# Early half expert with one PSUM bank and one product per attention iteration, four score banks throughout, and two loads moved ahead of the weights

## Chip, core and metric

The kernel runs on one core of a Trainium2 chip. The metric is the device time of one execution in microseconds (us); lower is better. TensorE is called PE here (PEld is its weight load), VectorE DVE, ScalarE ACT, GpSimd POOL; SP is the engine that issues most DMAs.

## What is computed

A causal attention with a decay bias, a mixture of eight experts that every token visits with its own weight, and a feed-forward block, one after the other, in float32.

```python
scores = scale * np.matmul(q, k.transpose(0, 1, 3, 2))        # 2 batches, 8 heads, 576 x 576, head_dim 64
scores = np.where(causal, -1000000000.0, scores + np.minimum(bias, 0.0))
attn = softmax(scores)
x = (attn @ v) as [1152, 512]
P = exp(x @ w_gate), then 8 rounds of row and column normalisation
for e in range(8):
    out += P[:, e:e + 1] * (np.maximum(x @ w1[e], 0.0) @ w2[e])     # 512 -> 1024 -> 512
h = out @ w_in                                                  # 512 -> 2048
y = (np.maximum(h, 0.0) + np.log1p(np.exp(-np.abs(h)))) @ w_out
```

## The kernel before

Every matrix is split into a high and a low part (`hi` rounded by ACT, `lo` the remainder on DVE or POOL) and every product is three matmuls on these parts. An expert's 1024 hidden units are handled as two half experts of 512, so the loop `for x in range(NH)` runs over 16 half experts and then 4 pieces of the feed-forward block. The tokens are two groups `g` of 576 (the two batches). For an expert, the first matrix product of a group is made by seven block products (Strassen's scheme, `Unit.product`, line 313, six matmuls of 288 columns each, into a PSUM tile `ph`); sums of them, relu and split give `hh` and `hl`. The second product, `downs` (line 449), takes tiles of 128 tokens: four steps of three 512-column matmuls into a PSUM tile `py`, which is then added to `acc`.

The attention comes first. Its unit is a pair of heads `p` (0 to 7, the first `NP` = 4 are batch 0) and a block `i` of 128 queries (0 to 3, and 4 for the last 64 rows of both heads). There are 40 units, and the loop over `n` is a software pipeline: iteration `n` issues the scores of unit n+1 (`do_S`), the transposes of unit n-3 (`do_T`), their copies to SBUF of unit n-4 (`do_V`), the product with v of unit n-5 (`do_A`), the softmax of unit n with the norm of unit n-2 (`do_B`, DVE), and the exponentials of unit n (`do_E`, ACT). The string `"YSKAXVWBMTED"` is the order in which these are written, so it sets the order on every engine's queue. Three more entries fill the pipeline: `W` prepares expert weights (`early_w`), `Y` builds the split x of group 0 from the finished attention of batch 0 (`build`), and `M` steps `early`, the generator of the first half expert's group 0 (`lone_half`, `Unit.lone`), from iteration 29 on.

PSUM has eight banks. Two (`tr`) hold transposes. `ring_bank` hands out the score banks: `s0`, `s1`, `s2`, `y0` in turn for pairs 0 to 3, but only the first three for pairs 4 to 7, two per unit; `y0` then holds `pv` (attention times v). `y1` and `y2` go to the early half expert: `lone` accumulates one chain of products in `y1` and puts the others in `y2`, copying partial sums from `y1` to the SBUF tile `xt`.

The loads of q and k for a pair (`load_qk`) go through SP's DMA queue, in the tiles `qk`, of which there are four. Pair 2's are issued when pair 0's last scores have been written, behind the four weight loads of 512 KB (`load`, line 158) and pair 1's v. `split_qk` makes the parts `kh`, `kl`, `qh`, `ql`; `split_ends` copies the last 64 columns of `qh` and `ql` to `end0h`... by DMA.

After the loop, `build` runs for group 1 while the rest of `early` is stepped, and the remaining steps go through `step()`. `step()` is called after each piece of the expert loop, and for x < 2 it advances `gates` (`gate_steps`) once in three calls and, from the seventh time on, once in seven. `gates` is the normalisation of P: a small matmul `pcs` (line 938) and some twelve DVE instructions on `gate`, `gs` and `csr` a round. What is left of it when x = 1 ends is run at once there (`for _ in gates: pass`).

Of the kernel before, what the change touches and what calls it, by code (L numbers as in the profile page):

```python
# [20 lines left out]
def attention_moe_ffn(ctx, tc, q, k, v, s, w_gate, w1, w2, w_in, w_out, out):  # L21
    nc = tc.nc
# [40 lines left out]
    def f(ap):  # L63
        return ap.bitcast(F32)
# [232 lines left out]
    class Unit:  # L297
# [23 lines left out]
        def lone(self):  # L321

            relu, sub = AF.Relu, ALU.subtract
            p = self.p

            def copy(n):
                nc.vector.tensor_copy(xt[:, n, :], a)

            def total_(n, z, m):
                nc.vector.tensor_tensor(out=xt[:, n, :], in0=z, in1=xt[:, m, :], op=ALU.add)  # L330

            def high(z, q, cols):
                nc.scalar.activation(out=hb[0][:, q, cols], in_=z, func=relu)

            def low(z, q, cols):
                nc.vector.scalar_tensor_tensor(out=hb[1][:, q, cols], in0=z, scalar=0.0, in1=f(hb[0][:, q, cols]),
                                               op0=ALU.max, op1=sub)

            a = bank("y1", "ph")[:, :HB]
            self.product(a, A11, B11, True)  # L340
            yield
            copy(0)
            b = bank("y2", "ph")[:, :HB]
            self.product(b, A12, B21, True)
            yield
            self.product(a, S2, T2, False)
            total_(2, b, 0)
            yield
            copy(1)
            high(xt[:, 2, :], p, self.h0)  # L350
            c = bank("y2", "ph")[:, :HB]
            self.product(c, S3, T3, True)
            yield
            self.product(a, S1, T1, False)
            low(xt[:, 2, :], p, self.h0)
            yield
            copy(0)
            total_(3, c, 0)
            self.product(a, S4, B22, False)
            yield  # L360
            high(xt[:, 3, :], p + 2, self.h1)
            self.product(c, A22, T4, False)
            high(a, p, self.h1)
            low(xt[:, 3, :], p + 2, self.h1)
            yield
            low(a, p, self.h1)
            total_(2, c, 1)
            high(xt[:, 2, :], p + 2, self.h0)
            low(xt[:, 2, :], p + 2, self.h0)

# [60 lines left out]

    def downs(x, groups):

        for tiles in groups:
            py = {}
            for t in tiles:
                nd[0] += 1
                py[t] = ps.tile([P, DM], F32, tag=f"y{1 + nd[0] % 2}", name="py", bufs=1)
            if x == XE:
# [34 lines left out]

    def lone_half():
        for p in range(2):
            yield from Unit(0, p, 0).lone()
            yield
        yield from downs(0, A_GROUPS)

    with tc.manual_schedule():
# [13 lines left out]
        with ExitStack() as att:  # L495
# [12 lines left out]
            def load_qk(n):  # L508

                p, r = divmod(n, 2)  # L510
                if p >= B * NP:
                    return
                b, hp = divmod(p, NP)
                x = ap2.tile([P, S], F32, tag="qk", name="qk", bufs=4)
                nc.sync.dma_start(out=x, in_=(q if r else k)[b, hp])
                qk_t.append(x)
# [108 lines left out]
            def scores(u):  # L625
                p, i = u
                t = pair.get(p)
                sc = [ring_bank("sc", 4 if p < NP else 3) for _ in range(2)]
                live[u] = dict(sc=sc)
# [24 lines left out]
            load_bias(1)  # L654
            nc.sync.dma_start(out=c8d, in_=f(cs))
            for which in (1, 2):
                for i in range(2):
                    load(0, which, i)
# [90 lines left out]
            def attend(u):  # L749
# [4 lines left out]
                if i == 0:  # L754
                    t["pv"] = bank("y1" if p < NP else "y0", "pv")
                if i < NB:
# [38 lines left out]
            def do_S(n):  # L795
                if unit(n + 1):
                    p, i = unit(n + 1)
                    scores((p, i))
                    if i == (0 if p else NB):
                        load_qk(2 * p + 4)  # L800
                        load_qk(2 * p + 5)
# [21 lines left out]
            def do_Y(n):  # L823
                for _ in range(3):
                    while building and next(building[0], 1):
                        building.pop(0)
# [19 lines left out]
            def do_D(n):  # L846
                if unit(n):
                    p, i = unit(n)
                    if i == NB - 1:
                        split_ends(p + 1)  # L850

            def do_W(n):
                for _ in range(0 if n < 9 else 1 if n < EARLY - 4 else 2):
                    next(prework, None)

            EARLY = NP * (NB + 1) + 9

            def do_M(n):
                for _ in range(0 if n < EARLY else 1 if n < nu + 3 else 2):
                    next(early, None)  # L860

            do = dict(S=do_S, T=do_T, V=do_V, A=do_A, X=do_X, Y=do_Y, B=do_B, E=do_E, K=do_K, D=do_D, W=do_W, M=do_M)
            for n in range(nu + LA + LX + 1):
                now[0] = n
                for x in "YSKAXVWBMTED":
                    do[x](n)
# [167 lines left out]
        def step(z=""):  # L1034
# [4 lines left out]
            if x < XE:  # L1039
                if tick[1] >= (3 if tick[3] < 6 else 7) and tick[2] > 2 and not dense[0]:  # L1040
                    next(gates, None)
                    tick[1] = 0
                    tick[3] += 1
# [146 lines left out]
```

## Time and profile before

| | us |
|---|---|
| three runs | 1117.37, 1120.87, 1120.93 |
| median | 1120.87 |
| profiled execution, device time | 1117.36 |
| its span (first to last instruction) | 1115.6 |
| busy in the span: PE, PEld, DVE, ACT, POOL | 1078.1, 953.1, 777.3, 517.5, 360.7 |

The span is cut into stages below by the start of a pair's first scores on PE: pair 1 at 16.40 us, pair 2 at 34.76, then 46.16, 57.56, 74.76, 91.50 and 110.09 for pair 7. The attention's last PE work ends near 141 us, and the experts and the feed-forward block fill the rest.

### The profile page before, as it was taken

The numbers are of one execution on the slowest core, as the hardware profiler recorded it, in microseconds if no ns is written. First come the engines' busy times: TensorE is split into PE (matmuls) and PEld (weight loads), VectorE is DVE, ScalarE is ACT, GpSimd is POOL, SyncE is SP. The second block draws the span as 40 slices with busy tenths as digits, with TensorE's granted clock in tenths as the row PEclk, the third lists the DMA queues.
The fourth block names the chain that finished last, engine by engine and source line by source line (L and its number), as shares of the span: only waits on it lengthen the run. The fifth ranks groups of instructions, "written<-read, shape, count | busy, mean of one in ns | idle before, by whom it ended". The sixth has DMA issues, their size and how long they took to land.

```text
span 1115.6 us, 18099 instructions
## 1 busy us (share of the span) xinstructions
PE 1078.1 (97%) x6692; PEld 953.1 (85%) x6692; DVE 777.3 (70%) x1727; ACT 517.5 (46%) x1227; POOL 360.7 (32%) x426
## 2 busy tenths in 40 slices
PE   5988999989999999999999999999999999999998
PEld 3766788878989899899989989889898889989997
DVE  5555464676877787887878888885545559687874
ACT  4887534332443343443433434434333357565662
POOL 5775321203424142342424324142130023233231
PEclk9999999999999999999999999999999999999999
DMA  5220201111323213232122312222011210121002
GB/s 191 72 73 31 71 2 38 38 49 65 130 79 114 96 67 111 79 133 95 67 95 95 132 66 97 95 76 85 20 57 38 76 39 1 41 74 38 1 1 85
DMA packets 30425, 78.50 MB, mean 70 GB/s; under 512 B 6048, under 2 KB 10656, under 8 KB 30336
## 3 DMA queue, kind: packets, MB, share of 16 engines
q1 hardware_dynamic: 27768, 68.93, 18.3%
q0 software_dynamic: 2560, 8.39, 1.9%
q8 instruction: 53, 0.87, 0.3%
q14 instruction: 36, 0.29, 0.1%
q10 hardware_dynamic: 8, 0.01, 0.0%
HBM read 66.00 MB, written 10.82 MB: 69 GB/s over the span
## 4 chain that ended last, share of the span: by engine, by line
PE 92%; DVE 4%; ACT 2%; DMA 1%; issue 1%; POOL 1%; ACTq 0%; POOLq 0%
PE py L449 43%; PE ph L313 32%; PE ph L424 9%; PE sc L647 2%; PE pv L759 2%; PE tr L733 1%; PE sc L651 1%; PE pv L769 1%; PE tr L727 1%; DVE xl L104 1%; DMA qk<-in_k 1%; ACT pt L747 1%; PE pg L915 0%; ACT eb L702 0%; ACT xh L101 0%
## 5 line engine op out<-in xcount | busy, mean ns | idle before, releaser
L449 PE MATMUL py<-w2h,hh 128*128 128x512 f32 x720 | 284.4, 395 | 1.9 <-DVE acc L464 1.6
L449 PE MATMUL py<-w2h,hl 128*128 128x512 f32 x720 | 282.6, 392 | 1.3 <-DVE hl L261 1.3
L449 PE MATMUL py<-w2l,hh 128*128 128x512 f32 x720 | 283.8, 394 | 0.0
L313 PE MATMUL ph<-xh,w1h 128*128 128x288 f32 x896 | 265.9, 297 | 0.0
L313 PE MATMUL ph<-xl,w1h 128*128 128x288 f32 x896 | 264.9, 296 | 0.0
L313 PE MATMUL ph<-xh,w1l 128*128 128x288 f32 x896 | 264.9, 296 | 0.0
L313 PEld LDWEIGHTS ph<-xh,w1h 128*128 128x128 f32 x896 | 168.8, 188 | 18.4 <-issue 1.7
L313 PEld LDWEIGHTS ph<-xl,w1h 128*128 128x128 f32 x896 | 169.0, 189 | 15.6
L318 ACT ACTIVATE xt<-ph 128x288 f32<-128x288 f32 x186 | 74.8, 410 | 206.0 <-PE ph L313 199.4
L313 PEld LDWEIGHTS ph<-xh,w1l 128*128 128x128 f32 x896 | 169.1, 189 | 0.0
L449 PEld LDWEIGHTS py<-w2h,hl 128*128 128x128 f32 x720 | 135.1, 188 | 33.5 <-DVE hl L261 2.4
L258 ACT ACTIVATE hh<-ph 128x288 fp32r<-128x288 f32 x186 | 76.0, 410 | 161.0 <-DVE ph L410 81.5
L449 PEld LDWEIGHTS py<-w2h,hh 128*128 128x128 f32 x720 | 135.1, 188 | 15.4 <-DVE acc L464 2.0
L449 PEld LDWEIGHTS py<-w2l,hh 128*128 128x128 f32 x720 | 135.1, 188 | 10.5
L224 POOL TENSOR_TENSOR w2l<-raw,w2h 128x512 fp32r<-128x512 f32 x40 | 56.2, 1405 | 269.7 <-ACT w2h L222 269.7
L467 DVE SCALAR_TENSOR_TENSOR acc<-py,gate,acc 128x512 f32<-128x512 f32 x126 | 93.9, 746 | 52.8 <-PE py L449 52.8
L998 POOL TENSOR_TENSOR cm<-cm,ct 128x512 f32<-128x512 f32 x32 | 44.9, 1402 | 209.3 <-DVE ct L996 209.3
L172 DVE TENSOR_TENSOR w1l<-raw,w1h 128x512 fp32r<-128x512 f32 (+1 forms) x144 | 98.5, 684 | 13.5 <-ACT w1h L169 13.3
L261 DVE SCALAR_TENSOR_TENSOR hl<-ph,hh 128x288 fp32r<-128x288 f32 x186 | 83.9, 453 | 29.7 <-ACT hh L258 28.1
L281 POOL TENSOR_TENSOR a<-a,a 128x288 f32<-128x288 f32 x64 | 51.7, 808 | 124.0 <-DVE a L279 121.8
L169 ACT ACTIVATE w1h<-raw 128x512 fp32r<-128x512 f32 (+1 forms) x144 | 82.9, 576 | 1.6 <-PE ph L313 1.6
L424 PE MATMUL ph<-xh,w1h 128*128 128x288 f32 x256 | 75.8, 296 | 0.0
(185 smaller groups left out, 1695.4 us busy)
## 6 DMA issues: line engine op xcount, KB each, us to landing
raw<-in_w SPq DMA_DIRECT2D x64, 512.0 KB
f<-in_w_in SPq DMA_DIRECT2D x16, 512.0 KB
f<-in_w_out SPq DMA_DIRECT2D x16, 512.0 KB
wd<-cm POOLq DMA_DIRECT2D x32, 256.0 KB, 2.9
raw<-wd SPq DMA_DIRECT2D x16, 512.0 KB
qk<-in_k SPq DMA_DIRECT2D x8, 288.0 KB
qk<-in_q SPq DMA_DIRECT2D x8, 288.0 KB
out<-acc SPq DMA_DIRECT2D x9, 256.0 KB
```

Source lines behind the costliest of these rows:

```text
L169: nc.scalar.activation(out=hi[:, o], in_=t[:, src], func=AF.Copy)
L172: nc.vector.tensor_tensor(out=lo[:, o], in0=t[:, src], in1=f(hi[:, o]), op=ALU.subtract)
L224: (nc.gpsimd if i else nc.vector).tensor_tensor(out=lo, in0=t[:, r], in1=f(hi), op=ALU.subtract)
L258: nc.scalar.activation(out=hh, in_=z, func=AF.Relu)
L261: nc.vector.scalar_tensor_tensor(out=hl, in0=z, scalar=0.0, in1=f(hh), op0=ALU.max, op1=ALU.subtract)
L281: nc.gpsimd.tensor_tensor(out=a2, in0=a1, in1=a2, op=ALU.subtract)
L313: nc.tensor.matmul(o, u, v, start=(start and c == 0 and n == 0), stop=(c == 1 and n == 2), skip_group_check=True)
L318: nc.scalar.activation(out=t, in_=self.a, func=AF.Copy)
L424: nc.tensor.matmul(o, u, v, start=(n == 0), stop=(n == 11))
L449: nc.tensor.matmul(py[t], u, v, start=(k == 0 and n == 0), stop=(k == NF - 1 and n == 2))
L467: nc.vector.scalar_tensor_tensor(out=a, in0=py, scalar=gate_t[0][:, t, e:e + 1], in1=a, op0=ALU.mult, op1=ALU.add)
L998: nc.gpsimd.tensor_tensor(out=m, in0=m, in1=f(t), op=ALU.add)
```

## The change

`lone` no longer accumulates in PSUM over several products: each of the seven products goes to bank `y2`, and its result is copied or added into one of four SBUF tiles `xt` by DVE. A `yield` now stands between the product and its eviction, and `M` stands twice in the string, ahead of `T` and behind it. So an iteration evicts the previous product in its first `M` and issues the next one in its second, behind the transposes; it starts at iteration 30. The scores use all four ring banks for every pair, and `pv` is always in `y1`. The down products of the early half take one tile at a time, with the banks `y2`, `y2`, `y1`, `y2`. Pair 2's q and k are loaded before the weights; for this pair 0's q and k lie in the buffers of `kh` and `qh`. `Y` takes two steps an iteration in place of three, `W` goes to two steps from iteration 28 in place of 25, and `step()` advances `gates` once in six calls in place of seven.

```diff
         def lone(self):
-            a = bank("y1", "ph")[:, :HB]
-            self.product(a, A11, B11, True)
-            yield
-            copy(0)
-            b = bank("y2", "ph")[:, :HB]
-            self.product(b, A12, B21, True)
-            yield
-            self.product(a, S2, T2, False)
-            total_(2, b, 0)
...
+            p, h0, h1 = self.p, self.h0, self.h1
+            o = [None]
+
+            def product(a, b):
+                o[0] = bank("y2", "ph")[:, :HB]
+                self.product(o[0], a, b, True)
+
+            def add(n, m):
+                nc.vector.tensor_tensor(out=xt[:, n, :], in0=o[0], in1=xt[:, m, :], op=ALU.add)
...
+            yield
+            product(A11, B11)
+            yield
+            nc.vector.tensor_copy(xt[:, 0, :], o[0])
+            yield
+            product(A12, B21)
+            yield
+            add(1, 0)
+            yield
+            product(S2, T2)
+            yield
+            add(2, 0)
+            high(1, p, h0)
...
+            product(A22, T4)
+            yield
+            add(2, 3)
+            high(1, p, h1)
+            low(0, p + 2, h1)
+            self.rest = [lambda: (high(2, p + 2, h0), low(1, p, h1)), lambda: low(2, p + 2, h0)]
-    def downs(x, groups):
-
+    def downs(x, groups, tags=()):
+
+        tags = iter(tags)
-                py[t] = ps.tile([P, DM], F32, tag=f"y{1 + nd[0] % 2}", name="py", bufs=1)
+                py[t] = bank(next(tags, f"y{1 + nd[0] % 2}"), "py")
     def lone_half():
+        rest = []
         for p in range(2):
-            yield from Unit(0, p, 0).lone()
-            yield
-        yield from downs(0, A_GROUPS)
+            u = Unit(0, p, 0)
+            for n, _ in enumerate(u.lone()):
+                if n and n % 2 == 0 and rest:
+                    rest.pop(0)()
+                yield
+            rest = u.rest
+        for z in rest:
+            yield
+            z()
+        yield
+        yield from downs(0, [(0,), (1,), (2,), (3,)], ("y2", "y2", "y1", "y2"))
-                x = ap2.tile([P, S], F32, tag="qk", name="qk", bufs=4)
+                tag, bufs = ("qk", 4) if p else ("kq"[r] + "h", 2)
+                x = ap2.tile([P, S], F32, tag=tag, name="qk", bufs=bufs)
-                sc = [ring_bank("sc", 4 if p < NP else 3) for _ in range(2)]
+                sc = [ring_bank("sc") for _ in range(2)]
             nc.sync.dma_start(out=c8d, in_=f(cs))
+            load_qk(4)
+            load_qk(5)
-                    t["pv"] = bank("y1" if p < NP else "y0", "pv")
+                    t["pv"] = bank("y1", "pv")
-                    if i == (0 if p else NB):
+                    if i == 0 and p:
-                for _ in range(3):
+                for _ in range(2):
                     while building and next(building[0], 1):
+            EARLY = (NP + 2) * (NB + 1)
+
             def do_W(n):
-                for _ in range(0 if n < 9 else 1 if n < EARLY - 4 else 2):
+                for _ in range(0 if n < 9 else 1 if n < EARLY - 2 else 2):
-            EARLY = NP * (NB + 1) + 9
-
             def do_M(n):
-                for _ in range(0 if n < EARLY else 1 if n < nu + 3 else 2):
+                if n >= EARLY:
                     next(early, None)
-                for x in "YSKAXVWBMTED":
+                for x in "YSKAXVWBMTMED":
-                if tick[1] >= (3 if tick[3] < 6 else 7) and tick[2] > 2 and not dense[0]:
+                if tick[1] >= (3 if tick[3] < 6 else 6) and tick[2] > 2 and not dense[0]:
```

How instructions move, at the three places that matter. First SP's DMA queue at the start of the attention, before and after (`raw` is a weight load, `vv` pair 1's v, `end1h` and `end1l` the pieces of pair 1's q):

```order
L655 DMA c8d<-xr 16x1152
L158 DMA raw_191<-in_w 128x1024
L158 DMA raw_193<-in_w 128x1024
L158 DMA raw_195<-in_w 128x1024
L158 DMA raw_197<-in_w 128x1024
L522 DMA vv<-in_v 128x4x128
L523 DMA vv<-in_v 64x128
L515 DMA qk<-in_k 128x576
L515 DMA qk<-in_q 128x576
L620 DMA end1h<-qh 64x64 x2
L620 DMA end1l<-ql 64x64 x2
```

```order
L671 DMA c8d<-xr 16x1152
L531 DMA qk<-in_k 128x576
L531 DMA qk<-in_q 128x576
L158 DMA raw_195<-in_w 128x1024
L158 DMA raw_197<-in_w 128x1024
L158 DMA raw_199<-in_w 128x1024
L158 DMA raw_201<-in_w 128x1024
L538 DMA vv<-in_v 128x4x128
L539 DMA vv<-in_v 64x128
L636 DMA end1h<-qh 64x64 x2
L636 DMA end1l<-ql 64x64 x2
```

The two `qk` loads, 0.59 MB, pass the four weight loads and pair 1's v; what follows is unchanged.

Second, DVE's queue behind the attention, where group 1's x is built (`xt`, `xl`) and the down products of the early half leave PSUM (`acc`), before and after:

```order
L104 TENSOR_TENSOR xl_1977<-xr,xh_1976 128x288
L461 COPY acc_87<-py 128x512
L98 TENSOR_TENSOR xt<-xr,xt 128x288
L104 TENSOR_TENSOR xl_1977<-xr,xh_1976 128x2x288
L98 TENSOR_TENSOR xt_1984<-xr,xt_1984 128x288
L104 TENSOR_TENSOR xl_1977<-xr,xh_1976 128x2x288
L461 COPY acc_88<-py 128x512
...
L104 TENSOR_TENSOR xl_1977<-xt_1984,xh_1976 128x4x288
L461 COPY acc_89<-py 128x512
L905 CAST wgs<-wg 128x4x8
```

```order
L104 TENSOR_TENSOR xl_1979<-xr,xh_1978 128x288
L467 COPY acc_87<-py 128x512
L98 TENSOR_TENSOR xt<-xr,xt 128x288
L104 TENSOR_TENSOR xl_1979<-xr,xh_1978 128x2x288
L98 TENSOR_TENSOR xt_1986<-xr,xt_1986 128x288
L104 TENSOR_TENSOR xl_1979<-xr,xh_1978 128x2x288
...
L104 TENSOR_TENSOR xl_1979<-xt_1986,xh_1978 128x4x288
L467 COPY acc_88<-py 128x512
L923 CAST wgs<-wg 128x4x8
```

The copy of tile 0 (`acc_87`) keeps its place; the copy of tile 1 (`acc_88`) moves behind all of the building.

Third, PE's queue at the end of half expert 1, where the last rounds of the gates stand. Before, two `pcs` stand back to back behind the last product of the old group and ahead of the next one's; the change has its last round 62 instructions ahead of that place:

```order
L313 MATMUL ph<-xh_74,w1l_2811 128x288
L938 MATMUL pcs<-csr,onesr 128x16 x2
L313 MATMUL ph<-xh_1976,w1h_2561 128x288
L313 MATMUL ph<-xl_1977,w1h_2561 128x288
L313 MATMUL ph<-xh_1976,w1l_2562 128x288
```

```order
L455 MATMUL py<-w2h_2481,hl 128x512
L956 MATMUL pcs<-csr,onesr 128x16
L313 MATMUL ph<-xh_74,w1h_2797 128x288
...
L313 MATMUL ph<-xh_74,w1l_2851 128x288
L313 MATMUL ph<-xh_1978,w1h_2587 128x288
L313 MATMUL ph<-xl_1979,w1h_2587 128x288
```

The eight rounds stand 25 to 28 PE instructions apart in the change, 25 to 58 before, and none is left for the end.

## Rows read from the trace of the kernel before

**Rows 1.** The page, part 1: an engine's busy time, share and instructions.

```profile
PE 1078.1 (97%) x6692; PEld 953.1 (85%) x6692; DVE 777.3 (70%) x1727; ACT 517.5 (46%) x1227; POOL 360.7 (32%) x426
```

**Rows 2.** Busy time by stretch, pairs 1 to 6 and 7: length, engines, clock.

```profile
core 0: us, PE busy (x) PEld busy (x) DVE busy (x) ACT busy (x) POOL busy (x), PEclk, DMA share, GB/s
16.40:34.76 18.36, 13.07 (x105) 9.79 (x105) 6.74 (x38) 10.53 (x31) 8.97 (x14) 0.81 0.53 183
34.76:46.16 11.40, 11.40 (x125) 8.85 (x125) 6.46 (x34) 10.96 (x32) 9.05 (x14) 1.00 0.29 88
...
57.56:74.76 17.20, 13.17 (x125) 9.77 (x125) 9.84 (x38) 13.57 (x36) 12.75 (x18) 0.93 0.19 58
74.76:91.50 16.74, 13.91 (x125) 10.18 (x125) 10.32 (x36) 13.59 (x36) 16.11 (x19) 0.91 0.29 91
91.50:110.09 18.59, 16.47 (x155) 13.62 (x155) 8.41 (x38) 12.55 (x35) 7.31 (x10) 0.96 0.08 21
110.09:128.76 18.67, 16.71 (x148) 13.75 (x147) 9.69 (x39) 12.22 (x34) 9.01 (x13) 0.91 0.34 105
```

**Rows 3.** Chain of waits, 14 to 160 us: start, length, what.

```profile
18.15 6.89 DMA qk<-in_k
...
32.31 1.05 PE sc L651 x8
...
93.46 0.99 PE ph L313 x6
```

**Rows 4.** PE's timeline at 26 us: start, length, instruction, idle before it.

```profile
26.27 1.09 PE L733 MATMUL tr<-ident,eb 128*128 128x128 f32 x4 [5.14 <-ACT pt L747]
```

**Rows 5.** SP's queue in order of time, 14 to 22 us.

```profile
14.35 1.84 SPq L158 DMA_DIRECT2D raw<-in_w  x4
...
19.27 1.16 SPq L620 DMA_DIRECT2D end1h<-qh  x2
```

**Rows 6.** DMA traffic from 12 to 32 us in 40 slices of 0.5 us.

```profile
GB/s 5 9 9 1 1 102 87 270 369 328 164 262 401 377 410 352 418 418 359 327 362 396 385 294 108 51 86 125 382 392 226 30 0 0 0 0 0 0 33 0
```

**Rows 7.** PE's waits from 57 to 141 us: total, times, longest.

```profile
PE sc L651 <- DVE st L680: 6.3, 3, 2.4
PE sc L647 <- DVE st L680: 4.6, 4, 2.0
```

**Rows 8.** Waits of the whole span: DVE for the early products.

```profile
DVE xt L327 <- PE ph L313: 6.1, 5, 2.1
```

**Rows 9.** Busy time by stretch, behind three waits: columns as in rows 2.

```profile
26.27:31.41 5.14, 5.14 (x28) 3.84 (x28) 1.21 (x5) 3.94 (x12) 3.88 (x6) 0.50 0.23 85
...
89.43:92.85 3.42, 3.42 (x34) 2.64 (x32) 1.94 (x13) 2.28 (x6) 1.75 (x3) 0.50 0.00 0
...
253.27:256.69 3.42, 3.42 (x16) 3.42 (x16) 1.31 (x6) 0.67 (x2) 2.07 (x4) 0.50 0.77 261
```

**Rows 10.** Timelines of DVE and of PE while group 1's x is built.

```profile
143.85 0.99 DVE L104 TENSOR_TENSOR xl<-xr,xh 128x288 fp32r<-128x288 f32 x1
146.03 0.69 DVE L461 COPY acc<-py 128x512 f32<-128x512 f32 x1 [1.20 <-PE py L449]
...
153.77 0.68 DVE L461 COPY acc<-py 128x512 f32<-128x512 f32 x1
...
154.82 0.31 PE L915 MATMUL pg<-xh,wgs 128*16 128x288 f32 x1 [1.39 <-DVE wgs L906]
```

**Rows 11.** PE's timeline at three places of half expert 1.

```profile
224.98 0.50 PE L449 MATMUL py<-w2h,hl 128*128 128x512 f32 x1 [0.98 <-DVE hl L261]
...
240.77 0.50 PE L449 MATMUL py<-w2h,hh 128*128 128x512 f32 x1 [1.60 <-DVE acc L464]
...
253.08 0.25 PE L938 MATMUL pcs<-csr,onesr 128*128 128x16 f32 x1 [4.00 <-DVE csr L951]
```

**Rows 12.** DVE's timeline: first instruction of a gate round, and the first behind it.

```profile
208.84 0.16 DVE L939 COPY gs<-pcs 128x8 f32<-128x8 f32 x1
...
211.56 0.69 DVE L172 TENSOR_TENSOR w1l<-raw,w1h 128x512 fp32r<-128x512 f32 x1
```

**Rows 13.** Chain of waits in half expert 1: pieces of PE at full pace.

```profile
241.74 0.80 PE ph L313 x6
242.53 1.40 PE py L449 x6
```

More of the change, by code (lines that the diff above doesn't have):

```diff
@@ L321, in lone @@
         def lone(self):
[L323 to L337, printed above, removed]
@@ L339, in lone, with high @@
-            a = bank("y1", "ph")[:, :HB]
-            self.product(a, A11, B11, True)
+            p, h0, h1 = self.p, self.h0, self.h1
[5 more added lines that the diff above has]
+                nc.vector.tensor_tensor(out=xt[:, n, :], in0=o[0], in1=xt[:, m, :], op=ALU.add)
+            def high(n, q, cols):
+                nc.scalar.activation(out=hb[0][:, q, cols], in_=xt[:, n, :], func=AF.Relu)
@@ L341, in lone, with low @@
+            def low(n, q, cols):
+                nc.vector.scalar_tensor_tensor(out=hb[1][:, q, cols], in0=xt[:, n, :], scalar=0.0,
+                                               in1=f(hb[0][:, q, cols]), op0=ALU.max, op1=ALU.subtract)
             yield
-            copy(0)
-            b = bank("y2", "ph")[:, :HB]
-            self.product(b, A12, B21, True)
+            product(A11, B11)
             yield
-            self.product(a, S2, T2, False)
-            total_(2, b, 0)
+            nc.vector.tensor_copy(xt[:, 0, :], o[0])
@@ L348, in lone @@
             yield
[L349 to L352, printed above, removed]
+            product(A12, B21)
             yield
-            self.product(a, S1, T1, False)
-            low(xt[:, 2, :], p, self.h0)
+            add(1, 0)
             yield
-            copy(0)
-            total_(3, c, 0)
-            self.product(a, S4, B22, False)
+            product(S2, T2)
             yield
-            high(xt[:, 3, :], p + 2, self.h1)
@@ L362, in lone @@
-            self.product(c, A22, T4, False)
-            high(a, p, self.h1)
-            low(xt[:, 3, :], p + 2, self.h1)
+            add(2, 0)
+            high(1, p, h0)
             yield
[L366 to L369, printed above, removed]
+            product(S3, T3)
+            yield
+            add(3, 2)
+            low(1, p, h0)
+            yield
+            product(S1, T1)
+            yield
@@ L371, in p1 @@
+            add(0, 3)
+            add(2, 2)
+            yield
+            product(S4, B22)
+            yield
+            add(1, 2)
+            high(0, p + 2, h1)
+            yield
[5 more added lines that the diff above has]
+            self.rest = [lambda: (high(2, p + 2, h0), low(1, p, h1)), lambda: low(2, p + 2, h0)]
         def p1(self):
```

## The prediction

> **What bounds the kernel now.** I read the page's busy times first: PE is busy 1078.1 of 1115.6 us [rows 1], so only some 37 us of the span are idle, and nothing that leaves PE's work as it is can win more than that, apart from time in which PE is busy at the lower of its two clock levels. Next, busy time by stretch, to find where the loss lies: pair 2 is 11.40 us long with PE busy all of it at a granted clock of 1.00, while pair 1 takes 18.36 at 0.81 and pairs 4 and 5 take 17.20 and 16.74 with the same 125 matmuls [rows 2]. So the attention is where an iteration can be shorter. Then the chain of waits and PE's timeline, for what ended each gap: a q and k load of 6.89 us in pair 1 [rows 3], a gap of 5.14 us behind it [rows 4], scores that wait for DVE to release a score bank in pairs 4 to 7 [rows 7], and three waits in half expert 1 [rows 11]. Behind such gaps stand stretches at a granted clock of 0.50, the 1.2 GHz level [rows 9]: each microsecond of such a stretch holds half the work, so it costs half its length. From half expert 2 on I found PE back to back; there the change touches nothing.
>
> The sum is made against the profiled execution: 1117.36 us, span 1115.6. The median of the three runs, 1120.87, lies 3.5 above.
>
> **A. Pair 2's q and k ahead of the weights.** In SP's queue the load now passes four 512 KB weight loads and pair 1's v [rows 5]. Between 16 and about 27 us the traffic runs at 300 to 400 GB/s without a break [rows 6], so the order of issue decides what lands when. Before, the load landed at 25.04 (18.15 + 6.89) [rows 3]; ACT, which works in order, held its next exponentials behind the copy of that k, and PE stood 5.14 us for them [rows 4] and then ran 5.14 us at 0.50 [rows 9], which costs 2.57. Both together are 7.7. Ahead of the weights, 0.59 MB at these rates take some 2 us, and the wait goes. What is late next: the `end1h`, `end1l` pieces, issued at 19.27 [rows 5] behind the same bytes as before. By the traffic the small pieces end near 25.5 to 26. Their scores stood at 32.31 [rows 3] and would come at 24.6, so some 1.5 us are given back. The v of pair 1 moves behind the q and k and is needed only five iterations on, so I cost it at nothing. **-6.2**; bounds -7.7 (pieces in time) and -4.5 (pieces at 27.5, where the last traffic ends).
>
> **B. Four score banks, pairs 4 and 5.** Before, 17.20 + 16.74 = 33.94 us. PE needs 2 x 11.40 = 22.8 at full pace, ACT was busy 27.16, POOL 28.86 [rows 2]. The waits of `sc` for DVE's `st`, 10.9 us over pairs 4 to 7 [rows 7], come from three banks shared by units that take two; pair 2, with four, shows none. With four banks the next bound is POOL and ACT. POOL can't be beaten below 28.86 unless its steps move; three steps of `W` go to pair 6 and `Y` takes two instead of three an iteration, which relieves it here. I take 30.2, nearer POOL's row than the old length, since POOL and ACT each still wait for the other at times. **-3.7**; bounds 0 (the engines' rhythm, not the banks, set the length) and -5.1 (POOL's busy time).
>
> **C. The same, pairs 6 and 7, with the early products.** Before, 18.59 + 18.67 = 37.26. Their 155 and 148 matmuls are 53 more than 2 x 125, nine products of six; a product is 0.99 [rows 3]. PE needs 22.8 + 9 x 0.99 = 31.7; the rest is ring waits and half clock (a stretch of 3.42 at 89.43 costs 1.7 alone [rows 9]). In the change one product fewer, or none fewer, stands ahead of the last scores. I take 33.0: the first unit behind pair 5 and one step late. **-4.3**; bounds -2.0 and -5.6 (PE's need).
>
> Each product of the early half now leaves PSUM at once, through the one bank `y2`. That adds two additions on DVE per half, of about the 0.46 us of the ones there; DVE was busy 8.41 of 18.59 and 9.69 of 18.67 [rows 2], so with half of it free I cost them at nothing; if that cover went they would be 1.8 for the two halves. The parts of hh and hl that are now split from SBUF instead of PSUM, the buffers of pair 0's q and k, `pv` in `y1`, and the steps of `Y` cost nothing for the same reason, POOL's 7.31 and 9.01 [rows 2] leaving room for the moved `W`.
>
> **D. One down tile at a time, banks y2, y2, y1, y2.** Before, tile 0's copy to `acc` stood at 146.03 after a wait for PE of 1.20, and tile 1 had its own bank [rows 10]. Now tile 1 shares `y2` and waits for that copy, which stands behind `xl` (143.85 + 0.99) and so ends near 145.7; PE is ready for tile 1 at about 143.8: 1.9 idle. Tile 3 waits for tile 1's copy, which now stands behind all of the building of group 1's x. That building runs from the end of one copy to 153.77 [rows 10], some 7.1 of DVE, while PE has eight steps of three matmuls, 8 x 0.70 = 5.6 (1.40 for six [rows 13]): 1.5 idle. The wait for `wgs`, 1.39 [rows 10], is swallowed in it. With one stretch at 0.50 like the 3.42 us ones [rows 9] behind two idle pieces, 1.7: 1.9 + 1.5 - 1.4 + 1.7 = 3.7. I take **+3.4**, the stretch being likely and not certain; bounds +1.5 (no such stretch, the first wait 0.5 shorter) and +5.4 (the wait for `wgs` stays, and the two others are 0.3 longer).
>
> **E. Gates once in six calls.** Before, half expert 1 lost 0.98 + 1.60 + 4.00 in three waits [rows 11] and 1.7 in the half-clock stretch behind the last [rows 9]: 8.3. The 4.00 is the rounds left over at the end, where two `pcs` stand back to back and PE has nothing ahead of the second until DVE finishes the round. With eight rounds done earlier that place is empty. A round costs DVE 2.72 us in one block (208.84 to 211.56) [rows 12], and it comes in every 25 to 28 PE instructions: 16 of `ph` and 10 of `py` are 16 x 0.80/6 + 10 x 1.40/6, some 4.5 us [rows 13]. That leaves DVE 1.8 us an interval for its other work, which by my count of its queue is about what stands there on average and twice that in one or two intervals. So the rate is just carried, with bursts: the 0.98 and 1.60 waits for six rounds become some 3.8 for eight. **-4.5**; bounds -1.0 (DVE late by 0.8 a round) and -7.0.
>
> Sum: -6.2 - 3.7 - 4.3 + 3.4 - 4.5 = -15.3, so 1102.1 for an execution like the profiled one. The median lies 3.5 higher; and two of the three runs lie there, so I add 2, a little more than half: **1104**.
>
> **Rivals.**
> *Banks were not the bound in pairs 4 to 7* (0.15). ACT and POOL set the rhythm, and four banks only move the wait to their results: for it, PE's waits for the banks are 10.9 [rows 7] while the four pairs stand 11.1 + 5.6 = 16.7 above PE's need; against, POOL's 7.31 of 18.59 in pair 6 [rows 2]. B and C give -2 together instead of -8: 1110.
>
> *The gates are too dense* (0.10). DVE, which also makes the splits of weights and of the hidden layer, falls behind from the third round on, and the waits add up before the end: E gives -1 to 0 and the time is 1108.
>
> *One bank serialises the early products* (0.05, the slower side). With `y2` alone each product waits until DVE has evicted the one before, and DVE has its softmax in the same queue. The price is one wait for each of the 14 products of the early half. From 16.9 / 14 = 1.2 us each it takes back all that separates 1104 from the median of before; that is also the mean of the waits seen between those two engines, 6.1 / 5, and the longest was 2.1 [rows 8]. At 1.7, midway, 24 us make it 1128. Against: DVE waited 6.1 us for PE's products, five times [rows 8], not PE for DVE, and the change puts DVE's softmax of a unit and the transposes between eviction and next product. The Trainium skill has a rule that speaks against the change here ("Perfetto Trace Analysis", Optimizing Tensor Performance, on matmuls): independent groups should rotate through PSUM banks, so that the eviction of one overlaps the matmuls of the next. By that rule this rival would hold and the time be its 1128; the trace bears it out only in part, since in this loop other PE work (scores, transposes) stands between two products.
>
> *Everything waited for goes* (0.12). No wait is put in place of the old ones: A -7.7, B -5.1, C -5.6, D +2, E -6.5, that is -22.9, and with the 2 of above 1096.5.
>
> *The load gets no earlier share* (0.03). If queues share the traffic rather than serve it in order, A is only -2: 1108.
>
> **Numbers.** The forecast has 0.55. The range takes in the first, second and last rivals and ends beyond the fourth: 1095 to 1112; outside are the slower case and the tails of the others. Some 0.3% (3.4 us) is what a measurement of this kernel can tell from no change. Faster needs less than 1117.5: all but the slower rival and a joint failure of two terms, 0.90; same 0.06, slower 0.04.
>
> **What would show it.** Right: pair 1 near 12 us, with no gap over 2 us at 20 to 27 us except before the scores of the `end1` pieces (A); pairs 4 to 7 near 15, 15, 16.5, 16.5 and no wait of `sc` for `st` (B, C); two waits of PE on `acc` while group 1's x is built, behind tiles 0 and 1 (D); no wait of 4 us for `csr` at the end of half expert 1, and small ones spread over its eight rounds (E). Wrong: PE's `ph` waiting for DVE's `xt` in pairs 6 and 7 shows the serial bank; pairs 4 and 5 above 16.5 with ACT or POOL in the chain show the first rival; `py` or `pcs` waits above 6 us in all in half expert 1 the second. If pair 1 keeps its gap, the forecast falls by 6.

## The result and the profile after

The change took 1102.06 us (median; 1097.9 to 1104.47 in four runs) against 1119.12 before, a ratio of 0.9848 with a 95% interval of 0.9803 to 0.9893. The forecast was 1104 in a range of 1095 to 1112, so the time and its sign came out; the sum behind it was right only in part: three of its five terms lie outside their own bounds, as the table below shows, and their misses nearly cancel. The profiled execution took 1100.33 us, with a span of 1098.5, 17.1 below the profiled execution of before.

The page, part 1, after the change (columns as in [rows 1]):

```profile
PE 1070.9 (97%) x6692; PEld 947.0 (86%) x6692; DVE 778.3 (71%) x1731; ACT 515.8 (47%) x1227; POOL 359.0 (33%) x426
```

PE has the same 6692 matmuls and is busy 7.2 us less than in [rows 1]: that part of the 17.1 is time in which it worked at the lower clock before. The other 9.9 was idle.

Busy time by stretch, after, columns as in [rows 2]: pairs 1, 2, 4, 5 and 6, and the rest up to the first down product of the early half.

```profile
16.30:31.43 15.13, 12.53 (x106) 9.26 (x105) 6.96 (x38) 10.65 (x31) 10.05 (x16) 0.89 0.69 230
31.43:42.83 11.40, 11.40 (x126) 8.86 (x125) 6.34 (x32) 10.92 (x32) 8.00 (x12) 1.00 0.29 88
...
54.21:66.18 11.97, 11.68 (x126) 8.93 (x125) 5.97 (x28) 11.65 (x35) 10.22 (x14) 1.00 0.28 83
66.18:82.54 16.36, 13.47 (x126) 9.88 (x125) 10.04 (x36) 13.63 (x36) 13.07 (x18) 0.90 0.29 93
82.54:98.61 16.07, 14.84 (x150) 12.02 (x149) 11.65 (x45) 13.06 (x38) 12.01 (x17) 1.00 0.09 25
98.61:125.72 27.11, 27.11 (x287) 22.82 (x286) 14.76 (x57) 18.47 (x50) 9.68 (x14) 1.00 0.22 73
```

Against [rows 2], pair 1 fell from 18.36 to 15.13 and still runs at a clock of 0.89. Pair 4 is near PE's own pace of 11.40 now, pair 5 is not. From pair 7 on to the first down product PE is busy without a gap.

PE's timeline after (start, length, instruction, idle before it and what ended it): the gap in pair 1, and then those of over 0.4 us from the first down product to the end of half expert 1:

```profile
27.17 0.38 PE L667 MATMUL sc<-kh,end1h 128*128 128x320 f32 x1 [2.46 <-DMA end1h<-qh]
...
130.41 0.50 PE L455 MATMUL py<-w2h,hh 128*128 128x512 f32 x1 [1.65 <-DVE acc L467]
...
138.46 0.50 PE L455 MATMUL py<-w2h,hh 128*128 128x512 f32 x1 [2.32 <-DVE acc L467]
...
198.33 0.50 PE L455 MATMUL py<-w2h,hh 128*128 128x512 f32 x1 [1.22 <-DVE acc L470]
...
210.29 0.25 PE L956 MATMUL pcs<-csr,onesr 128*128 128x16 f32 x1 [0.48 <-DVE csr L969]
...
211.02 0.50 PE L455 MATMUL py<-w2h,hh 128*128 128x512 f32 x1 [0.48 <-ACT hh L258]
...
216.21 0.25 PE L956 MATMUL pcs<-csr,onesr 128*128 128x16 f32 x1 [0.53 <-DVE csr L969]
```

The gap of 5.14 [rows 4] has become one of 2.46 for `end1h`; the 4.00 for `csr` [rows 11] has gone; the two waits on `acc` are new. All PE waits of over 0.3 us between pair 2 and the first wait on `acc` (what waited for what, total, times, longest):

```profile
PE sc L663 <- DVE st L708: 2.1, 2, 1.4
PE py L455 <- DVE acc L467: 1.6, 1, 1.6
PE tr L745 <- POOL eb L733: 0.8, 2, 0.5
PE tr L745 <- ACT pt L765: 0.6, 1, 0.6
PE tr L751 <- POOL eb L733: 0.5, 1, 0.5
PE tr L751 <- ACT xr L837: 0.4, 1, 0.4
```

The waits of scores for DVE, 10.9 in [rows 7], are 2.1, and no product `ph` waits for `xt`. Of the gain in pairs 4 and 5, 5.2 us lie in pair 4 (17.20 to 11.97) and only 0.4 in pair 5 (16.74 to 16.36), where 15 each was forecast.

By stage, from the same instruction to the same instruction (pair starts by their first scores; the last stage ends at DVE's first gated `acc`, 265.50 before and 247.69 after; the forecast's C ended a little sooner, with no difference expected behind it):

| stage | before | after | difference | forecast (bounds) |
|---|---|---|---|---|
| A, pair 1 | 18.36 | 15.13 | -3.2 | -6.2 (-4.5 to -7.7) |
| B, pairs 4 and 5 | 33.94 | 28.33 | -5.6 | -3.7 (0 to -5.1) |
| C, pair 6 to the first down product | 49.49 | 43.25 | -6.2 | -4.3 (-2.0 to -5.6) |
| D and E, to the end of half expert 1 | 124.58 | 121.97 | -2.6 | -1.1 |

The four make -17.6, pairs 2 and 3 did not move, and the remaining 0.5 lies in the start and the last output.

### The profile page after: what moved, and what is told of

It is laid out like the page before. It is cut to its first block, busy times and chain, and to the rows that moved or that the text cites. A ratio compares the mean times of both kernels' runs of the same rounds, so it can differ in the third digit from the quotient of the medians.

```text
span 1098.5 us, 18109 instructions
## 1 busy us (share of the span) xinstructions
PE 1070.9 (97%) x6692; PEld 947.0 (86%) x6692; DVE 778.3 (71%) x1731; ACT 515.8 (47%) x1227; POOL 359.0 (33%) x426
## 4 chain that ended last, share of the span: by engine, by line
PE 92%; DVE 4%; ACT 1%; DMA 1%; POOL 1%; issue 1%; SPq 0%; ACTq 0%; POOLq 0%; DVEq 0%
PE py L455 44%; PE ph L313 32%; PE ph L429 9%; PE sc L663 2%; PE pv L777 2%; PE tr L751 1%; DVE xl L104 1%; PE sc L667 1%; DMA end1h<-qh 1%; ACT eb L720 1%; PE pg L933 0%; PE tr L745 0%; POOL eb L733 0%; PE pv L787 0%; DMA qk<-in_k 0%
```

## The experiments

Each was timed beside the kernel before, which had medians of 1117.5 to 1118.5 us there, and is one edit on the changed kernel if not said otherwise. Ratios are to the kernel before, with their 95% interval; stages and rows are of one execution each. Line numbers in rows shift by a few.

**undo_qk.** The load of pair 2's q and k at its old place.

```diff
-            load_qk(4)
-            load_qk(5)
...
-                    if i == 0 and p:
+                    if i == (0 if p else NB):
```

> The change with pair 2's q and k load back at its old place, behind the weights and pair 1's v. Theory (the load's place in SP's queue is what shortened pair 1): pair 1 goes from 15.1 us back to about 18.4, a gap of some 5 us on PE returns ahead of the transposes, and the time is 3.2 us over the change's 1102.1, about 1105. Rival (pair 1 became shorter by the other buffers or the other order, or the load's early landing is worth its full 7.7): pair 1 stays near 15, time within 1 us of 1102; or pair 1 at 20 or more, time 1108 and above.

1103.48 us (0.9872 of before, 0.9857 to 0.9887). Busy time of pair 1, and PE's gap in it:

```profile
15.80:34.10 18.30, 12.57 (x106) 9.36 (x105) 6.71 (x38) 10.53 (x31) 9.44 (x15) 0.81 0.60 197
```

```profile
26.14 1.94 PE L749 MATMUL tr<-ident,eb 128*128 128x128 f32 x8 [5.63 <-ACT pt L763]
```

Pair 1 is back at 18.3 and the gap too, 3.2 us over the change's 15.13; the median is only 1.4 over, within what executions of the change differ by. The stage speaks for the theory. The load's place is worth 3.2 against the change's profiled execution, and neither nothing nor 7.7 against any other: the five further executions below that have the change's instructions in pair 1 (three_banks, wy_old, gates7, gates7_later, down_banks) take 12.8 to 16.4 there, so 1.9 to 5.5 less than the 18.3 here.

**w_late.** The four weight loads behind the pieces `end1h` and `end1l`.

```diff
-            for which in (1, 2):
-                for i in range(2):
-                    load(0, which, i)
...
                         split_ends(p + 1)
+                        if p == 0:
+                            for which in (1, 2):
+                                for z in range(2):
+                                    load(0, which, z)
```

> The change with the four weight loads (2.1 MB) issued behind the pieces end1h and end1l in SP's queue instead of ahead of them. Theory (in pair 1 the pieces now wait behind the bytes of the weights): they land some 3 us earlier, PE's wait of 2.46 us for end1h and the stretch at half clock behind it (3.8 us, costing 1.9) both go, pair 1 is about 11 us long, and the time is 4.3 us below the change, 1097.8. Rival (the pieces are slow by themselves, or the weights are late for the first steps of W and ACT waits for them ahead of pair 2): pair 1 keeps over 14 us or pair 2 grows by as much; time within 1 us of 1102.

1101.0 us (0.9842, 0.9821 to 0.9863): no difference from the change that its interval can show. Pairs 1 and 2 apart, and the gap in pair 2:

```profile
15.77:26.51 10.74, 10.70 (x104) 8.09 (x103) 6.71 (x37) 10.21 (x31) 9.38 (x15) 1.00 0.85 297
26.51:43.72 17.21, 14.80 (x125) 11.29 (x124) 6.21 (x33) 11.31 (x32) 9.39 (x14) 0.80 0.26 84
```

```profile
29.18 0.29 PE L663 MATMUL sc<-bk,bq 64*128 64x128 f32 x1 [2.17 <-DMA bq<-c8d]
```

Both were right. Pair 1 runs at full pace as soon as the four weight loads no longer stand ahead of the 16 KB pieces (pair 2's q and k and pair 1's v still do): what was left of the old loss was bytes in the queue. But the same bytes then stood ahead of pair 2's bias rows of 4.5 KB, and 5.8 us came back there. The Trainium skill ("DMA: Bandwidth & Descriptors", Queues, rings and completion order) says that each DMA engine takes a queue's descriptors in their order; these two runs agree, with 2.46 us of waiting for the one small piece and 2.17 for the other.

**w_bias.** Behind the pieces now pair 2's bias rows, one weight load, pair 3's q and k, and then the other three weight loads.

```diff
-            for which in (1, 2):
-                for i in range(2):
-                    load(0, which, i)
...
                         load_qk(2 * p + 5)
+                        if p == 1:
+                            for which, z in ((1, 1), (2, 0), (2, 1)):
+                                load(0, which, z)
...
                         split_ends(p + 1)
+                        if p == 0:
+                            load_bias(2)
+                            load(0, 1, 0)
...
-                        if p > 0:
+                        if p > 1:
                             load_bias(p + 1)
```

> The change with SP's queue reordered behind the pieces end1h and end1l: pair 2's bias rows first, then the first weight load, pair 3's q and k, then the other three weight loads. The run with all weights behind the pieces had pair 1 at 10.7 us instead of 15.1, but pair 2 at 17.2 instead of 11.4, because the bias rows (bq) stood behind the weights. Theory (pair 1's loss is bytes ahead of small pieces, wherever they stand): pair 1 about 10.8, pair 2 about 11.4 to 12.5, the span 3.5 to 4.4 us below the change's, time about 1098. Rival (the bytes only move: now a weight or pair 3's k is late for the first step of W or the next split, and the engine in order behind it stops): pair 2 or 3 grows by 3 us or more, time within 1.5 us of 1102.

1097.75 us (0.9811, 0.9787 to 0.9835).

```profile
16.57:27.43 10.86, 10.72 (x105) 8.11 (x104) 6.83 (x37) 10.35 (x31) 8.88 (x14) 1.00 0.70 233
27.43:38.82 11.39, 11.39 (x125) 8.85 (x124) 6.46 (x33) 10.96 (x32) 9.06 (x14) 1.00 0.50 168
```

Both pairs run at PE's pace: 4.3 us under the change's 15.13 + 11.40. The theory holds; nearly the whole 7.7 that I had priced could be had (pair 1 from 18.36 to 10.86), but by the order of the queue, not by the one load.

**three_banks.** Three score banks in pairs 4 to 7, `pv` still in `y1`.

```diff
-                sc = [ring_bank("sc") for _ in range(2)]
+                sc = [ring_bank("sc", 4 if p < NP else 3) for _ in range(2)]
```

> The change with three score banks in pairs 4 to 7 as before; all else as in the change. Theory (the bank ring was the bound there): PE waits again for DVE's st ahead of the scores, some 10 us over pairs 4 to 7, and the time is 8 to 11 us over the change, 1110 to 1113. Rival (ACT and POOL set the rhythm, and the moved steps of W and Y made the gain): pairs 4 and 5 stay below 30 us together, and the time is at most 3 us over the change, 1102 to 1105.

1109.45 us (0.9923, 0.9909 to 0.9936), 7.4 over the change. PE's waits from pair 4 to the first wait on `acc`, with the totals:

```profile
PE sc L663 <- DVE st L708: 5.9, 2, 3.3
PE sc L663 <- DVE st L698: 2.3, 3, 0.9
```

Pairs 4 to 6 take 52.3 us (52.25 to 104.54) against 44.4 in the change. The waits are 8.2 rather than 10, the time is just below the theory's lower end, and far above the rival's: the ring was the bound in pairs 4 to 6. Pairs 4 and 5 take 33.1 here and took 33.94 before, pair 6 takes 19.2 and took 18.59. From pair 7 to the first down product it was not: there is no wait for `st`, and it takes 27.18 as in the change, against 30.90 before.

**wy_old.** Three steps of `Y` an iteration, two of `W` from iteration 25.

```diff
-                for _ in range(0 if n < 9 else 1 if n < EARLY - 2 else 2):
+                for _ in range(0 if n < 9 else 1 if n < EARLY - 5 else 2):
...
-                for _ in range(2):
+                for _ in range(3):
                     while building and next(building[0], 1):
```

> The change with Y at three steps an iteration and W at two steps from iteration 25, as before. Theory (with four banks the rest of the loss in pairs 4 and 5 is the work of Y and W on ACT, DVE and POOL, so their pace matters): pairs 4 and 5, 28.3 us in the change, take 29.5 to 32, pair 6 is unchanged at 16 or 0.5 shorter, and the time is 1 to 3 us over the change, 1103 to 1105. Rival (four banks alone set these lengths): pairs 4 and 5 within 0.7 us of 28.3, time within 0.7 of 1102.

1103.74 us (0.9869, 0.9848 to 0.9890). Pairs 4 and 5 take 29.8 (54.21 to 84.00), 1.5 more, but PE idles no longer in them: a longer stretch at half clock, 1.7, accounts for it, and such a stretch also differs between executions of one kernel. What is clear comes later: PE waits for products, which it does nowhere in the change.

```profile
PE ph L313 <- DVE xt L331: 1.0, 1, 1.0
PE ph L313 <- DVE st L729: 0.5, 1, 0.5
```

The time lies where the theory had it, but 1.7 over the change is within what executions of the change differ by, and the place is only partly the one it named.

**gates7.** The gates once in seven calls.

```diff
-                if tick[1] >= (3 if tick[3] < 6 else 6) and tick[2] > 2 and not dense[0]:
+                if tick[1] >= (3 if tick[3] < 6 else 7) and tick[2] > 2 and not dense[0]:
```

> The change with the gates advanced once in seven calls as before. Theory (the rounds left over at the end of half expert 1 cost the wait): a wait of PE for csr of about 4 us returns there with a stretch at half clock behind it, the waits spread over the half expert shrink by about 1, and the time is 4 to 5 us over the change, 1106 to 1107. Rival (the earlier start, not the density, emptied the end): no wait over 1 us at the end, time within 1 us of 1102.

1099.35 us (0.9835, 0.9817 to 0.9853): the theory falls. There is no wait at the end; from the first down product to the first gated `acc` it takes 121.3 us, 0.7 less than with six. The rival has the place right and not the time: 2.7 under the change, where within 1 was expected, is more than the stage gives and within what executions of the change differ by.

**gates7_later.** The same, begun three calls later.

```diff
-        tick = [0, 0, 0, 0]
+        tick = [0, -3, 0, 0]
```

> The change with the gates once in seven calls and begun three calls later, which puts their eight rounds at the places they had before, the last two back to back at the end of half expert 1. With seven in place of six but the earlier begin, the run above showed no wait there. Theory (the begin, which the change shifts by one call, removed the wait, and the six or seven calls did not): the wait of about 4 us for csr is back with a stretch at half clock behind it (1.7), and the time is 5 us over the run with seven calls, 1104 to 1105. Rival (something else of the change made DVE quicker there): the wait is below 1.5 us and the time at most 1101.

1107.2 us (0.9905, 0.9889 to 0.9921). The last `pcs` of both on PE, gates7 first:

```profile
236.79 0.17 PE L956 MATMUL pcs<-csr,onesr 128*128 128x16 f32 x1
```

```profile
242.60 0.35 PE L956 MATMUL pcs<-csr,onesr 128*128 128x16 f32 x1 [4.01 <-DVE csr L969]
```

Begun later, the wait of 4.0 is back to a hundredth, with a stretch at half clock behind it (242 to 246, costing 1.7). So with seven calls the earlier begin empties the end. The change shifts it by three calls of `step()`, one of `gates`, without saying so: in it eight steps of three `py` of the early half are left over when group 1's x is built, five before, and each goes through a call of `step()`. So the first `pg` stands ahead of the last six `py` in the change and behind all of them, and six `ph`, before. From the first down product to the first gated `acc` it takes 128.7 us, 7.4 over gates7 where 5 was expected: 4.01, 1.7, and another 1.7 of half clock behind the wait of 2.28 on `acc`, which gates7 has without one.

**down_banks.** A bank for each early down tile.

```diff
-        yield from downs(0, [(0,), (1,), (2,), (3,)], ("y2", "y2", "y1", "y2"))
+        yield from downs(0, [(0,), (1,), (2,), (3,)], ("y2", "y0", "y1", "s2"))
```

> The change with a bank of its own for each of the four down tiles of the early half (y2, y0, y1, s2; the score banks are free by then). Theory: the two waits of PE on acc (1.65 and 2.32 us in the change) go, but PE then waits for DVE's wgs, which stands behind the building of group 1's x and ended near 138.7, so the first pg comes only 1.3 us earlier than its 139.96: time 1.3 us below the change, 1100.8. Rival (the two waits are the whole price of one tile at a time): 4 us less, 1098, with no wait for wgs over 0.5 us.

1100.63 us (0.9843, 0.9821 to 0.9866), no difference that its interval can show.

```profile
141.94 0.31 PE L933 MATMUL pg<-xh,wgs 128*16 128x288 f32 x1 [3.23 <-DVE wgs L924]
```

The two waits on `acc` go, 3.97 in all, and 3.23 come back at the next late thing: DVE's `wgs` behind the building, as in [rows 10]. The first `pg` comes 13.07 us behind the first down product instead of 14.24, 1.2 earlier as the theory has it, and a stretch at half clock behind the longer wait takes that back.

**best1, best2, best3: together.** best1 is w_bias with the banks of down_banks and seven calls; best2 has six calls, begun three calls later, which puts six more `py` and six `ph` ahead of the first `pg`; best3 is best2 with `W` pausing in iterations 24 and 25 and doubled only from 31.

> The reordered SP queue, four banks for the early down tiles, and the gates once in seven calls (which took no longer than six in the run above), together. Theory (the three lie in different stages and add): -4 for pair 1, -1.3 while group 1's x is built, 0 to -0.7 for the gates, so 5.3 to 6 us below the change, about 1096.5. Rival (time won ahead is waited out at the next late thing: DVE's building or wgs): at most 3 us below the change, 1099 or more.

1097.19 us (0.981, 0.9788 to 0.9832), 4.9 under the change, between theory and rival: it adds next to nothing to w_bias, since the wait of 3.23 for `wgs` stands there as well.

> The reordered SP queue, a bank of its own for each early down tile, gates once in six calls and begun three calls later, so that six py and six ph stand ahead of the first pg. Theory (with own banks PE stood 3.23 us for wgs and then ran at half clock for some 3 us because it had nothing ahead of pg; 2.2 us of other work there shorten the stop to 1 and may spare the half clock): from the first py to the end of half expert 1 it takes 2 to 3.8 us less than with the reordered queue alone, time 1094 to 1096. Rival (another wait takes its place, for the xl of group 1's x, or the gates end later and PE waits for them at the end of half expert 1): at most 0.7 us less, time 1097 or more.

1095.93 us (0.9797, 0.9782 to 0.9813), the lowest median here, 1.8 under w_bias; the two intervals overlap, so the stage has to tell.

```profile
137.08 0.31 PE L936 MATMUL pg<-xh,wgs 128*16 128x288 f32 x1 [1.67 <-DVE wgs L927]
...
233.12 0.17 PE L959 MATMUL pcs<-csr,onesr 128*128 128x16 f32 x1
```

The stop shrinks to 1.67, no half clock follows it, and the way from the first down product to the first gated `acc` is 120.5 us instead of 122.0: 1.5 less, short of the 2 to 3.8 expected. The later begin does not bring the wait of 4 back: the last `pcs`, at 233.12, has no wait, since with six calls only one round is left for the end of the half expert, and no two stand back to back.

> The fastest run so far (reordered SP queue, own banks for the early down tiles, gates begun three calls later), and W pauses in iterations 24 and 25 and takes two steps only from iteration 31 instead of 28. Theory (the w1l and raw steps of W stand ahead of DVE's softmax and POOL's eb in pairs 5 and 6; with them later the score banks come free earlier): the waits for st (1.41 and 1.16 us) fall below 0.8 each, at least one stretch at half clock there goes, pairs 5 and 6 together take 31 to 32.7 us instead of 34.2, time about 1093.5. Rival (the waits there are set by xl and the norms, not by W, or the weights come late for the second early unit): pairs 5 and 6 within 0.8 us of 34.2 or PE waits for w1 in pair 7, time 1095 to 1098.

1096.53 us (0.9819, 0.9805 to 0.9833): the same as best2. Pairs 5 and 6 do fall, from 34.2 to 31.6 (61.25 to 92.89), but from there to the first down product it takes 29.6 instead of 27.2. One place of that:

```profile
111.33 0.40 PE L313 MATMUL ph<-xh,w1h 128*128 128x288 f32 x1 [1.23 <-DVE xt L331]
```

DVE, shortly before, in the same run (its columns as PE's):

```profile
108.95 0.69 DVE L224 TENSOR_TENSOR w2l<-raw,w2h 128x512 fp32r<-128x512 f32 x1 [1.40 <-ACT w2h L222]
...
110.83 0.45 DVE L331 TENSOR_TENSOR xt<-ph,xt 128x288 f32<-128x288 f32 x1
```

A step of `W` that was put off waits there for ACT, with the softmax and the eviction behind it in DVE's queue, and the product waits for its bank. In wy_old the `w2l` ahead of the late eviction waited 2.33 for ACT in the same way. The gain was given back.

**y_behind.** w_bias with `Y` written behind the softmax.

```diff
-                for x in "YSKAXVWBMTMED":
+                for x in "SKAXVWBYMTMED":
```

> The reordered SP queue (1097.8), and besides Y, which builds group 0's x, written behind the softmax of an iteration instead of ahead of all. Theory (in pair 5 DVE comes late to the score banks because the xl of Y, 1.36 us, stands ahead of the softmax; PE waits 1.41 us for st and then runs at half clock): that wait falls below 0.5 us, pair 5, 16.4 us, becomes 2 to 3 us shorter, and the time is about 1095.5. Rival (DVE, ACT and POOL together have too much work there, in any order): the wait moves to another place of pair 5 or 6, both together stay within 1 us of 34.1, time 1097 to 1098.5.

1098.02 us (0.9823, 0.9809 to 0.9837); pairs 5 and 6 take 34.1 as before. The wait for `st` is gone, and the one for POOL's `eb` at the end of pair 5, 1.15 in w_bias, has grown:

```profile
77.94 0.68 PE L742 MATMUL tr<-ident,eb 128*128 128x128 f32 x2 [2.85 <-POOL eb L730]
```

The rival holds for these two orders: the wait only moves. Of the three engines POOL is the full one here, busy 16.07 of pair 5's 16.56 us, with ACT at 14.2 and DVE at 12.2.

## Why the prediction was right, and where not

**A was too large, outside its bounds.** The mechanism was right (undo_qk), its size not. The failed step is what I gave back, "some 1.5 us", from pieces that land at 25.5 to 26. They landed at 27.03, the wait was 2.46, and behind it stood a stretch at half clock, 27.8 to 31.2, that costs 1.7 and that I had left out. 7.7 less 2.46 and 1.7 is 3.5; measured were 3.2. w_late and w_bias show what the pieces waited for. The size is that of one execution. In the six with this queue the pieces landed at 26.2 to 27.6, later than forecast in all of them, and PE waited 1.38 to 3.24. Pair 1 of three_banks, where the wait is the shortest and no half clock follows (16.70 on), and the longest wait, of down_banks:

```profile
16.70:29.50 12.80, 11.18 (x106) 8.09 (x105) 6.81 (x37) 10.26 (x31) 8.82 (x13) 1.00 0.77 262
```

```profile
27.44 0.60 PE L667 MATMUL sc<-kh,end1h 128*128 128x320 f32 x1 [3.24 <-DMA end1h<-qh]
```

Pair 1 came out 2.0 to 5.5 below the 18.36 of before in these six, and only three_banks, the 5.5, reaches the bounds.

**B was too small, outside its bounds.** The step that failed is the floor: I stopped near POOL's 28.86 [rows 2], "unless its steps move". POOL is busy 10.22 + 13.07 = 23.3 in the two pairs now, and pair 4 reached 11.97. The moved steps of `W` and `Y` are part of it: with their old pace POOL has 26.0 in wy_old, which leaves the other 2.9 unexplained. That the ring was the bound was right (three_banks).

**C was too small, outside its bounds.** The term that failed is the product's 0.99 [rows 3], one that ran partly at the lower clock; in the change's chain of waits they stand like this:

```profile
91.14 0.79 PE ph L313 x6
```

Nine of them need 1.8 us less than I took, which is nearly the whole miss of 1.9. Two things qualify it. In w_late and down_banks the same stage takes 45.0 instead of 43.25, with a stretch at half clock in it that costs 1.7 and that this execution does not have; there the gain is 4.5, near the forecast. And the fourth bank won only pair 6: what took the wait of 1.96 and the half clock of 1.7 behind it out of pair 7, where before they made the 3.7 that it is shorter now, is not the bank (three_banks). Before, in pair 7:

```profile
115.15 0.39 PE L647 MATMUL sc<-kh,qh 64*128 64x256 f32 x1 [1.96 <-DVE st L680]
```

Which other part of the change did it, the half expert taken one product at a time or the moved `W`, was not tested alone. The stretch at 89.43 that the forecast counted here lay for 2.07 of its 3.42 us in pair 5.

**D came nearly as worked out.** The waits were 1.65 and 2.32 where 1.9 and 1.5 were forecast, the 1.39 for `wgs` went: +2.6. The half-clock stretch of 1.7 did not come in this execution; in gates7_later and wy_old, with the same two waits, it did. The 1.65 was the price of the shared bank; the second wait, as down_banks shows, only stands where one for `wgs` would be.

**E was right, but its cause is one of two.** Waits and half clock of half expert 1 fell from 8.3 to 1.22 + 0.48 + 0.48 + 0.53 = 2.7, so -5.6 where -4.5 was forecast. The end is empty with six calls and the old begin (best2, with other edits ahead of it) and with seven and the earlier one (gates7); only seven with the old begin has the wait, 4.00 before and 4.01 in gates7_later. So "once in six calls" would have done it, as forecast. The change also begins the gates earlier, which does it as well; I had seen that in the order of the queue and put it down to the wrong line of the diff. With the earlier begin six calls cost 0.7 over seven (121.97 against 121.31, and 122.39 in down_banks against 121.74 in best1).

**The rivals.** Banks were the bound, so the first fell; the gates were carried, so the second fell; new waits came in place of the old ones (1.65, 2.32 and 2.46), so the fourth did; the load's place mattered (undo_qk), so the last did. *One bank serialises the early products* did not happen here: PE waited for no eviction. It is near, though: 1.0 us in wy_old and 1.2 in best3, where a `w2l` that waited for ACT stood ahead of the eviction. So the rule of the Trainium skill that independent groups should rotate through PSUM banks ("Perfetto Trace Analysis", Optimizing Tensor Performance) did not bind for the products, which have transposes and scores between them; for the down tiles, which follow each other directly, it did: 1.65 and 2.32 us.

That the total came out 2 us from the forecast is luck in part: the misses of A, B and C, +3.0, -1.9 and -1.9, nearly cancel.

## What to carry to other kernels

A small load that someone waits for should stand ahead of the large ones in its queue, and then the next small one has to be looked for: each step that was taken only moved the wait until all small pieces stood in front. One PSUM bank was enough here for a chain of products, since other matmuls lie between two of them; where something long stood ahead of the eviction on its engine, it was not. A table or a counter that is driven by calls moves when the number of calls moves, so its effect has to be tested apart from the constant beside it, and the two together: each of them alone emptied the end here.

## What was not expected of the hardware

Stretches of half clock decide much of what one execution differs from another. Summed over slices of 1 us between 10 and 300 us as one less the granted clock, before lost 10.2 us to them, the change 3.4, down_banks 10.2 and best3 nothing, mostly in steps of 1.7. The change's two, busy time of PE and clock:

```profile
27.80:31.20 3.40, 3.40 (x24) 0.51 0.05 16
72.00:75.40 3.40, 3.40 (x21) 0.53 0.84 285
```

Both lie behind gaps (2.46, and 1.41 with others). But the same gaps do not always bring one: the waits on `acc` brought none in the change and one in gates7_later. The change's four executions have mean clocks of 0.998, 0.996, 0.992 and 0.990 and spans of 1096.0, 1098.5, 1101.2 and 1102.7: nearly 7 us, more than most of the single edits are worth. That is why edits are read here from their stage first and from the median second, and why a stage of a single execution, pair 1's above all, is no exact size either.
